# Attention and two MLPs in one kernel: the matmuls of constants get a PSUM bank of their own, the weights' scratch shrinks to one bank, and the ranks are set anew

## The chip, the cores and the metric

The kernel runs on one core of a Trainium2 chip. The metric is the device time of one execution in microseconds. The engines are TensorE (PE in the rows), its weight loads (PEld), VectorE (DVE), ScalarE (ACT), GpSimd (POOL) and SyncE (SP, which issues most DMAs).

## The reference

Softmax attention over 4 batches, 8 heads, 576 positions and a head size of 64, in which scores below the row's maximum minus `tau` are dropped before the exponential. Its output, 2304 tokens by 512, goes through two MLPs of width 2048, one after the other, with no residual.

```python
scores = scale * np.matmul(q, k.transpose(0, 1, 3, 2))
thresh = np.max(scores, axis=-1, keepdims=True) - tau
scores = np.where(scores >= thresh, scores, -1000000000.0)
attn = softmax(scores)                       # exp(scores - max) / (sum + 1e-9)
x = (attn @ v) as [tokens, heads * head_dim]
h = x @ w_in1;  x = (h * np.clip(h + 3.0, 0.0, 6.0) / 6.0) @ w_out1
h = x @ w_in2;  x = (h - np.tanh(h)) @ w_out2
```

Everything is float32. The kernel splits a float32 operand into two halves of 16 bits and adds up three products, so what TensorE does in layer 1 and 2 is three times the plain number of matmuls.

## The kernel before

**Stages.** Up to about 530 us attention runs in 144 units. A unit is one head and 128 queries (a rest of 64 queries for two heads makes a unit of its own): four score matmuls (line 717) into a tile of two PSUM banks, the row maxima on VectorE (722), the exponential on ScalarE (724), the threshold (727 on ScalarE for the first 30 units, 730 on VectorE after that), the mask on VectorE (733). For two or three units together the result is cut into high and low halves (738 on ScalarE, 744 on GpSimd), turned by a DMA transpose (747) and multiplied with the values (770). The transposing of keys, queries and values on TensorE (589, 605, 656) and their splitting (612, 614, 619, 621, 654 to 672) go on beside it. When half a batch (256 or 320 tokens) is through, its x is normed (797 to 807), its scale found (`x_scale`, 819 to 823: a transpose, a maximum, a spread to all partitions, and a power of two on VectorE at 475 to 479), and it is transposed and split (852 to 857).

Layer 1 runs over such halves of batches in passes: a pass is one half of a batch and one half of the 2048 hidden columns. `PASSES` lists ten passes that run beside attention; six more (`ENDING`) follow it, and then layer 2. A pass has eight hidden blocks (516, gates at 870 to 885) and four output blocks (958). A pass needs its weights: each of 16 weights of the first half of hidden columns is loaded into one of three staging tiles (426, 431), made absolute on ScalarE (437) and clamped on GpSimd (441), and put together from 64 bits on VectorE in three steps (446, 449, 452) that use a PSUM bank of `R_m` as scratch. When all eight of a kind are there, their norms give the scale (1028 to 1038), and they are split into halves (1047, 1049). The second half of the weights goes the same way later.

**Order.** No engine's order is written by hand. Each piece of work is a task with an engine, a guessed duration, what it depends on and a key. `Plan.issue` plays through the program with these durations: each engine that is free takes the task with the lowest key among those that are ready, and the instructions are issued in the order so found. On the chip each engine works through its list in that order and waits where data isn't there. So a key is a rank, not a time. Unit u has the key T0 + 3.0 u + 0.8 min(u, 4). Pass p starts at a key of its own: at least FO x 3.0 behind the key of the last unit that it needs (plus five), and at least FW behind the pass before it. The first weights have T0 + 3.0 (W0 + 0.8 n), their scaling WAL later and WAP apart; the second half's weights begin with unit WB0.

**PSUM.** There are eight banks: two tiles of two banks for scores (`R_s`), two banks for transposes and small products (`R_tp`), and two banks `R_m`, which layer 1 uses for its products and which the weights use as scratch. `R_m` is a free ring: a task that needs a bank takes whichever of the two is free by the plan's times.

**Fillers.** When the plan finds TensorE free with nothing ready, before `until` (470 us by the plan's time), and TensorE's planned work of late is under a share of 0.55, it puts in two matmuls of constants (line 688). They write the columns 288 to 511 of the two banks of the score tile that was written last; scores take 0 to 287 of each. Each instruction's waits follow from the tiles that it touches, so a filler waits for the readers of that tile and they for it. At the start 24 of them are issued at once.

Of the kernel before, what the change touches and what calls it, by code (L numbers as in the profile page):

```python
# [15 lines left out]
BF16 = mybir.dt.bfloat16  # L16
# [57 lines left out]
class Plan:  # L74
# [13 lines left out]
    def add(self, eng, dur, key, fn, r=(), w=(), after=(), xfer=0.0, hold=False, slack=0.0, port=None):  # L88
        r, w = ([getattr(b, "of", b) for b in x] for x in (r, w))
        deps = dict.fromkeys(after)  # L90
        for b in r:
            deps.update(dict.fromkeys(b.writers))
        t = Task(eng, dur, key, fn, deps, xfer, hold, slack, eng == "pool" if port is None else port)
        t.w = w
        users = dict.fromkeys((*r, *w))
        t.free = [b for b in users if b.ring.free]
        for b in users:
            b.users.append(t)
        for b in w:
            b.writers.append(t)  # L100
        self.tasks.append(t)
        return t
# [97 lines left out]
def t_act(n, sbuf=False, scalars=False):  # L200
    return 0.05 + n / 1200.0 + 0.043 * sbuf + 0.094 * scalars
# [6 lines left out]
def t_pool(n):  # L208
    return 0.14 + n * 0.0021
# [3 lines left out]
def attention_moe_moe_kernel(  # L213
# [41 lines left out]
    SH = S // 2  # L255
# [11 lines left out]
    plan = Plan()  # L267
    add = plan.add

    LAG = 4  # L270
    STEP, SLOW, KNEE = 3.0, 0.8, 4
    LK, LQ, LV, LD = 5, 2, 1, 4
    XL, FO = 1, 6.1
    FW = 35.6
    W0, WS, WO = 7.2, 0.8, -2.0
    PVK, GK, RK = -7.0, -5.0, -2.6
    T2O = 0.0
    PASSES = [(0, 0, 0), (0, 1, 0), (1, 0, 0), (0, 0, 1), (1, 1, 0), (0, 1, 1), (2, 0, 0), (1, 0, 1), (2, 1, 0), (3, 0, 0)]
    CLAMP, LOD = True, (8, 8)
# [4 lines left out]
    F0, EK, CL, P2L, CF = 2.0, 4.0, 0.2, 22.0, 1.0  # L284
    NF, SF, PACE, PREP, PW, TK = 18, 14, 11.0, 2, 55.0, 40
    PK, PREP0 = (100.0, 90.0), 1
    T0 = 10.2
    WB0, WBS, WBD, WBL, WBP = 34, 2, 0.8, 6.1, 3.0
    WAL, WAP = 7.0, 1.82
    ZU, TAIL = 30, 3  # L290
    ST, SB, CS = 5.3, 2.9, 0.0
    SHARE, UNTIL, FIRST_FILL = 0.55, 470.0, 24
    LG, LX, LR = 0.0, 0.0, 0.0


# [29 lines left out]
    ones = const.tile([128, 128], F32, name="ones")  # L325
# [18 lines left out]
    def at_ring(*a):  # L344
        at_rings.append(ring(*a))
        return at_rings[-1]

    R_s = at_ring(ps_s, 2, [128, 2, 512], F32, "s")
# [47 lines left out]
    R_m = Ring(2, lambda i: ps_m.tile([128, 512], F32, tag=f"m{i}", name="m"), free=True)  # L396
# [142 lines left out]
    NU = len(units)  # L539
# [139 lines left out]
        return QT[b, g, j].t[:, part, h % 2, c % 2 * 128:c % 2 * 128 + 128]  # L679

    GT, XT = {}, {}
    scored = [None]

    def filler(n=2):

        spare = scored[0].t[:, :, SH:512]
        for i in range(n):
            nc.tensor.matmul(  # L688
                spare[:, i % 2], ones.bitcast(BF16)[:, 0:128], ones.bitcast(BF16)[:, 0:512 - SH], start=True, stop=True)

    def sum_group(u):

        b, g, j, h, c = units[u]
        if h is None:
            return [u]
        return [x for x in (u - 1, u, u + 1) if 0 <= x < NU and units[x][:4] == (b, g, j, h)]

    def softmax(u, key):

        b, g, j, h, c = units[u]  # L700
        ps, z = R_s.new(), R_z.new()
        hs = (h,) if h is not None else (2 * j, 2 * j + 1)
        us = sum_group(u)
        if u == us[0]:
            GT[u] = R_e.new(), R_pp.new(), R_pt.new()
        (e, pp, pt), n = GT[us[0]], u - us[0]
        s = lambda: ps.t[:, :, 0:SH]
        ex = lambda: e.t[:, n, :].rearrange("p (a s) -> p a s", a=2)

        def scores():  # L710
            scored[0] = ps
            if u == NU - 1:
                plan.until = 0.0
            ops = [(queries(b, g, j, x, c, part), KS[b, j].t[:, x % 2]) for x in hs for part in range(2)]
            for i, (l, ks) in enumerate(ops):
                for half in range(2):
                    nc.tensor.matmul(  # L717
                        ps.t[:, half, 0:SH], l, ks[:, half * SH:(half + 1) * SH], start=i == 0, stop=i == len(ops) - 1,
                    )

        add("pe", 0.53 * len(hs), key, scores, r=[KS[b, j], QT[b, g if h is not None else "l", j]], w=[ps])
        add("dve", 0.69, key, lambda: nc.vector.tensor_reduce(  # L722
            out=z.t[:, 0:1], in_=s(), axis=AX.XY, op=ALU.max, negate=True), r=[ps], w=[z])
        exp = add("act", 0.66, key, lambda: nc.scalar.activation(  # L724
            out=ex(), in_=s(), func=ACTF.Exp, bias=z.t[:, 0:1]), r=[ps, z], w=[e])
        if u < ZU:
            add("act", 0.2, key, lambda: nc.scalar.activation(
                out=z.t[:, 1:2], in_=z.t[:, 0:1], func=ACTF.Identity, scale=-1.0, bias=tau_b[:, 3:4]), r=[z], w=[z], after=[exp])
        else:
            add("dve", 0.15, key, lambda: nc.vector.tensor_scalar(  # L730
                out=z.t[:, 1:2], in0=z.t[:, 0:1], scalar1=-1.0, scalar2=tau_b[:, 1:2],
                op0=ALU.mult, op1=ALU.subtract), r=[z], w=[z])
        add("dve", 0.74, key, lambda: nc.vector.scalar_tensor_tensor(  # L733
            out=ex(), in0=s(), scalar=z.t[:, 1:2], in1=ex(), op0=ALU.is_ge, op1=ALU.mult),
            r=[ps, e, z], w=[e])
        if u == us[-1]:
            w = len(us)
            high = add("act", t_act(w * S, sbuf=True), key, lambda: nc.scalar.activation(  # L738
                out=pp.t[:, 0:w, 0:S], in_=e.t[:, 0:w, :], func=ACTF.Copy), r=[e], w=[pp])

            for src, dst in ((slice(SM, S), slice(S, S + LF)), (slice(0, SM), slice(S + LF, 2 * S))):
                ln = w * (src.stop - src.start)
                eng, dur, queue = ("pool", t_pool(ln), nc.gpsimd) if u < NU - TAIL else ("dve", t_dve(ln), nc.vector)
                add(eng, dur, key, lambda src=src, dst=dst, queue=queue: queue.tensor_tensor(  # L744
                    out=pp.t[:, 0:w, dst], in0=e.t[:, 0:w, src], in1=pp.t[:, 0:w, src], op=ALU.subtract),
                    r=[e], w=[pp], after=[high])
            add("dma", 0.65, key, lambda: nc.sync.dma_start_transpose(
                out=pt.t[:, 0:w].rearrange("p u k n -> p (u k) n"), in_=pp.t[:, 0:w].rearrange("p u s -> p (u s)")),
                r=[pp], w=[pt], xfer=1.63 * w, hold=True)
        return pt  # L750
# [65 lines left out]
    def x_scale(b, g, key):  # L816

        hb = 2 * b + g
        x = add("dve", 0.15, key, lambda: nc.vector.tensor_reduce(
            out=xtop[:, hb:hb + 1], in_=xsq[:, hb, 0:2 + g], axis=AX.X, op=ALU.max), after=x_done[b, g])  # L820
        x = highest(xtop[:, hb:hb + 1], one[0:1, hb % 4:hb % 4 + 1], key + 0.1, [x], R_tp, LX)
        x = everywhere(one[0:1, hb % 4:hb % 4 + 1], key + 0.1, [x], R_tp, 0.45, lambda bank: root(
            bank, xpow[:, 0, hb:hb + 1], xpow[:, 1, hb:hb + 1]), LX)
        x_scaled[b, g] = x

    def x_unscale(b, g, half, key):

# [139 lines left out]
    with tc.manual_schedule():  # L967
# [7 lines left out]
        nc.vector.tensor_scalar(out=tau_b[:, 3:4], in0=tau_b[:, 1:2], scalar1=-1.0, scalar2=None, op0=ALU.mult)  # L975
        nc.vector.memset(three[:, 0:1], 3.0 * GS)
        nc.vector.memset(xsq.rearrange("p b i -> p (b i)"), 0.0)
        plan.idle, plan.until, plan.share = filler, UNTIL, SHARE
        ps0 = R_s.new()

        def first():
            scored[0] = ps0
            filler(FIRST_FILL)

        add("pe", 0.19 * FIRST_FILL, -100.0, first, w=[ps0])
        for t in vt_t:
            for i in range(2):
                nc.gpsimd.memset(t[:, i, :, :, D:D + 1].rearrange("p h c d -> p (h c) d"), 1.0 - i)
# [16 lines left out]

        when = lambda u: T0 + STEP * u + SLOW * min(u, KNEE)
        W1, staged, w_scaled, w_found = {}, {}, {}, {}
# [82 lines left out]
        for u in range(NU + LAG + XL + 4):  # L1090
# [8 lines left out]
            if w_parts[0]:  # L1099
                kind, m = w_parts[0].pop(0)  # L1100
                n = 2 * MH - len(w_parts[0]) - 1
                key = T0 + STEP * (W0 + WS * n + WO * (kind == "o"))
                weight(0, kind, m, key, 0.8, slack=ST, scratch=R_m, cs=CS)
# [7 lines left out]
        start = 0.0  # L1111
# [9 lines left out]
        for b, g, half in PASSES:  # L1121
            if half == 0:
                start = max(start, when(last_unit[b, g] + LAG + XL) + FO * STEP)
                x_rounds(b, g, start - FO * STEP)
            layer1(b, g, half, start, FW)
            start += FW
        for b, g in last_unit:
# [47 lines left out]
        key = T2  # L1175
        steps, hid, before, count = [], [], {}, [0]
        for x, (b, g, half) in enumerate(ENDING):
# [14 lines left out]
            for ms in groups:  # L1192
                ps = (R_m, R_h)[count[0] % 2].new()
# [3 lines left out]
                for a, m in enumerate(ms):  # L1197
                    turn[:] = [add("pe", P, key + a * P, lambda a=a, m=m, ps=ps, n=n, half=half, xT=xT, c=len(ms): mm3(
                        ps.t[:, a * n:(a + 1) * n], in_pairs(W1[half, "i", m], xT.t, slice(0, n)),
                        first=a == 0, last=a == c - 1),  # L1200
# [296 lines left out]
        for idx, st in enumerate(order2):  # L1497
# [36 lines left out]
            if p < NP2:  # L1534
# [6 lines left out]
                ps, k_, then = piece(0, "A11", "X11")  # L1541
                s1 = keep(ps, k_)
                then()
                ps, k_, then = piece(1, "S2", "T2")
# [3 lines left out]
                ps, k_, then = piece(2, "A12", "X21")  # L1548
# [3 lines left out]
                ps, k_, then = piece(3, "S1", "T1")  # L1552
# [3 lines left out]
                ps, k_, then = piece(4, "S4", "X22")  # L1556
# [3 lines left out]
                ps, k_, then = piece(5, "S3", "T3")  # L1560
# [4 lines left out]
                ps, k_, then = piece(6, "A22", "T4")  # L1565
# [4 lines left out]
            else:  # L1570
                a, b = R_m.new(), R_m.new()
# [55 lines left out]
```

## Time and profile before

| | us |
|---|---|
| median of 3 runs | 1082.66 |
| these runs | 1080.37 to 1085.33 |
| the profiled execution | 1079.7 |
| its span, first to last instruction | 1077.9 |
| TensorE busy | 1016.5 (94%) |
| VectorE busy | 808.4 (75%) |
| ScalarE busy | 723.9 (67%) |
| GpSimd busy | 355.2 (33%) |
| fillers on TensorE, 374 matmuls | 52.4 |

Busy time is an average over stages. To read it for this change the span has to be cut: the stage up to the first pass of layer 1 (118 us), the stretch in which attention and layer 1 run together, and the rest, in which TensorE alone is left. TensorE's busy time includes the fillers, so real work is the one less the other. An idle time that a row names in front of an instruction is put down to the instruction on another engine that came last before it.

### The profile page before, as it was taken

To read this page: it belongs to the slowest core of one execution; us is meant where nothing else is said; L and a number is where in the kernel's file an instruction comes from. 1 tells how busy PE (TensorE), PEld (TensorE's weight loads), DVE (VectorE), ACT (ScalarE), POOL (GpSimd) and SP (SyncE) were. 2 spreads that over 40 slices of the span, in tenths; PEclk is the share of its full clock that TensorE was granted. 3 is DMA by queue.
4 is the path that set the end of the run, shared out by engine and by line. 5 is a ranking of instruction groups with operands and counts; after the bars stand their busy time and mean duration, and the time that the engine had idled before them with its cause. 6 is when DMAs were issued, how large, how long until landed. Compare 5 with 4: busy or idle time off the path is not lost.

```text
span 1077.9 us, 24007 instructions
## 1 busy us (share of the span) xinstructions
PE 1016.5 (94%) x9293; PEld 780.7 (72%) x9293; DVE 808.4 (75%) x1625; ACT 723.9 (67%) x1347; POOL 355.2 (33%) x377
## 2 busy tenths in 40 slices
PE   7667996999999999999999999999999999999998
PEld 5556885778988788898786787776576666666664
DVE  5878899989688577886547896478987796784664
ACT  6757787897998677886555774457756674574332
POOL 3544546786867465765320000000001111111000
PEclk9998999999999999999999999999999999999999
DMA  7788779998768766786648664133234856574335
GB/s 184 169 191 176 148 165 199 209 206 168 150 151 166 149 135 141 140 147 140 132 146 290 215 217 138 58 104 134 90 124 132 206 133 109 127 128 52 87 90 144
DMA packets 284946, 161.48 MB, mean 150 GB/s; under 512 B 203168, under 2 KB 261024, under 8 KB 284832
## 3 DMA queue, kind: packets, MB, share of 16 engines
q1 hardware_dynamic: 279024, 150.25, 56.3%
q0 software_dynamic: 5184, 9.44, 6.4%
q8 instruction: 73, 1.20, 0.5%
q14 instruction: 41, 0.34, 0.1%
q10 hardware_dynamic: 624, 0.26, 0.1%
HBM read 76.02 MB, written 41.42 MB: 109 GB/s over the span
## 4 chain that ended last, share of the span: by engine, by line
PE 79%; DVE 9%; ACT 6%; DMA 3%; issue 2%; POOL 1%; SPq 0%; ACTq 0%; DVEq 0%
PE ya L516 23%; PE m L516 22%; PE h L516 9%; PE m L958 8%; PE s L717 6%; PE tp L770 5%; PE s L688 3%; DVE z L722 2%; PE tp L589 2%; ACT e L724 2%; DMA pt<-pp 2%; DVE e L733 1%; DVE ks L614 1%; ACT wo L1047 1%; DVE m L449 1%
## 5 line engine op out<-in xcount | busy, mean ns | idle before, releaser
L516 PEld LDWEIGHTS <-wo 128*128 128x128 f16 x2112 | 201.2, 98 | 57.4 <-issue 1.7
L744 POOL TENSOR_TENSOR pp<-e,pp 128x128 f16<-128x128 f32 (+3 forms) x156 | 180.5, 1177 | 120.1 <-issue 57.5
L516 PE MATMUL ya<-wo,g 128*128 128x512 f16 x864 | 205.4, 379 | 2.5 <-DVE g L882 1.3
L516 PEld LDWEIGHTS <-wi 128*128 128x128 f16 x1536 | 149.7, 98 | 39.6
L516 PE MATMUL m<-xT,wo 128*128 128x256 f16 (+1 forms) x1248 | 168.8, 285 | 2.5 <-DVE t L872 1.5
L1447 POOL DMA_DIRECT2D po<-o x36 | 31.3, 876 | 410.6 <-ACT o L1441 410.6
L516 PEld LDWEIGHTS <-g 128*128 128x128 f16 x864 | 83.5, 98 | 82.3 <-DVE g L882 3.1
L733 DVE SCALAR_TENSOR_TENSOR e<-s,z,e 128x576 f32<-128x576 f32 x144 | 116.5, 812 | 29.0 <-ACT e L724 19.6
L722 DVE TENSOR_REDUCE z<-s 128x1 f32<-128x576 f32 x144 | 107.7, 751 | 35.4 <-PE s L717 31.6
L958 PE MATMUL m<-g,wo 128*128 128x256 f16 (+1 forms) x960 | 128.7, 284 | 1.3 <-ACT y L903 0.6
L724 ACT ACTIVATE e<-s,z 128x576 f32<-128x576 f32 x144 | 105.6, 737 | 30.9 <-DVE z L722 19.1
L878 ACT ACTIVATE g<-t 128x512 f16<-128x512 f32 (+1 forms) x168 | 94.3, 565 | 41.9 <-DVE t L1414 24.6
L958 PEld LDWEIGHTS <-wo 128*128 128x128 f16 x960 | 89.3, 98 | 22.9 <-issue 1.8
L717 PE MATMUL s<-ks,q 128*128 128x288 f32 x512 | 101.3, 322 | 4.0 <-DVE e L733 3.7
L738 ACT ACTIVATE pp<-e 128x1152 f16<-128x1152 f32 (+1 forms) x80 | 85.0, 1062 | 15.9 <-DVE e L733 15.1
L516 PE MATMUL m<-x,wi 128*128 128x256 f16 x768 | 94.9, 273 | 0.0
L1412 ACT ACTIVATE t<-t,hid_s 128x512 f32<-128x512 f32 x72 | 51.6, 719 | 62.8 <-DVE t L1403 62.3
L770 PE MATMUL tp<-vt,pt 128*128 128x65 f16 (+1 forms) x2240 | 83.4, 195 | 10.0 <-ACT x L777 2.9
L770 PEld LDWEIGHTS <-pt 128*128 128x128 f16 (+1 forms) x2240 | 78.5, 101 | 18.4 <-issue 13.0
L717 PEld LDWEIGHTS s<-ks,q 128*128 128x128 f32 x512 | 74.6, 193 | 10.0 <-DVE e L733 5.8
L688 PE MATMUL s<-ones 128*128 128x224 bf16 x374 | 52.4, 283 | 26.9 <-ACT e L724 15.0
L516 PE MATMUL ya<-g,wo 128*128 128x320 f16 (+1 forms) x576 | 77.5, 290 | 0.0
(166 smaller groups left out, 1631.2 us busy)
## 6 DMA issues: line engine op xcount, KB each, us to landing
st<-in_moe_w_in_dram SPq DMA_DIRECT2D x32, 512.0 KB, 4.6
st<-in_moe_w_out_dram SPq DMA_DIRECT2D x32, 512.0 KB, 4.6
po<-o POOLq DMA_DIRECT2D x36, 256.0 KB, 4.2
ys<-y SPq DMA_DIRECT2D x32, 160.0 KB, 2.1
y<-ys SPq DMA_DIRECT2D x9, 512.0 KB, 5.3
po<-o SPq DMA_DIRECT2D x18, 256.0 KB, 2.0
o<-po SPq DMA_DIRECT2D x18, 256.0 KB, 3.3
kr<-in_k_dram SPq DMA_DIRECT2D x16, 256.0 KB, 3.8
```

What stands on the lines that cost most here:

```text
L516: nc.tensor.matmul(ps, l[a], r[b], start=first and t == 0 and i == 0, stop=last and t == 2 and i == n - 1,)
L688: nc.tensor.matmul(spare[:, i % 2], ones.bitcast(BF16)[:, 0:128], ones.bitcast(BF16)[:, 0:512 - SH], start=True, stop=True)
L717: nc.tensor.matmul(ps.t[:, half, 0:SH], l, ks[:, half * SH:(half + 1) * SH], start=i == 0, stop=i == len(ops) - 1,)
L722: add("dve", 0.69, key, lambda: nc.vector.tensor_reduce(out=z.t[:, 0:1], in_=s(), axis=AX.XY, op=ALU.max, negate=True), r=[ps], w=[z])
L724: exp = add("act", 0.66, key, lambda: nc.scalar.activation(out=ex(), in_=s(), func=ACTF.Exp, bias=z.t[:, 0:1]), r=[ps, z], w=[e])
L733: add("dve", 0.74, key, lambda: nc.vector.scalar_tensor_tensor(out=ex(), in0=s(), scalar=z.t[:, 1:2], in1=ex(), op0=ALU.is_ge, op1=ALU.mul ...
L738: high = add("act", t_act(w * S, sbuf=True), key, lambda: nc.scalar.activation(out=pp.t[:, 0:w, 0:S], in_=e.t[:, 0:w, :], func=ACTF.Copy), ...
L744: add(eng, dur, key, lambda src=src, dst=dst, queue=queue: queue.tensor_tensor(out=pp.t[:, 0:w, dst], in0=e.t[:, 0:w, src], in1=pp.t[:, 0: ...
L770: nc.tensor.matmul(pv.t[0:m, w_ * (D + 1):(w_ + 1) * (D + 1)], pt.t[:, n, blk, rows], vv, start=o == 0, stop=o == len(ops) - 1)
L878: hi = add("act", t_act(n, sbuf=True), key, lambda: nc.scalar.activation(out=gh(), in_=t(), func=ACTF.Copy, scale=GS2 if far else 1.0), r= ...
L958: prev = [add("pe", t_half(n, 1), kd, lambda o=o, l=l, r=r, m=m, s=s, ps=ps, gt=gs[m // 2]: nc.tensor.matmul(ps.t[:, 0:n], W1[half, "o", m ...
L1412: add("act", t_act(2 * NB, sbuf=True, scalars=True), key, lambda: nc.scalar.activation(out=s_(), in_=h.t, func=ACTF.Tanh, scale=c), r=[h], ...
```

## The change

The fillers write columns 0 to 223 of one tile `unread`, which is taken from `R_m` at the start and which nobody reads. It is held until a last task, which issues one more filler, sets `until` to 0 and runs once the scale of the first half batch's x is found; no filler is put in after it. Until then `R_m` has one bank left, so the weights' three steps share that one. A group of constants is set anew. Among them T0 is a summand of all keys of units, weights and passes.

```diff
-    LK, LQ, LV, LD = 5, 2, 1, 4
-    XL, FO = 1, 6.1
-    FW = 35.6
-    W0, WS, WO = 7.2, 0.8, -2.0
-    PVK, GK, RK = -7.0, -5.0, -2.6
+    LK, LQ, LV, LD = 5, 2, 2, 4
+    XL, FO = 1, 9.2
+    FW = 34.4
+    W0, WS, WO = 7.3, 0.8, -2.0
+    PVK, GK, RK = -6.8, -5.0, -2.6
...
-    T0 = 10.2
-    WB0, WBS, WBD, WBL, WBP = 34, 2, 0.8, 6.1, 3.0
-    WAL, WAP = 7.0, 1.82
+    T0 = 8.4
+    WB0, WBS, WBD, WBL, WBP = 36, 2, 0.8, 6.1, 2.2
+    WAL, WAP = 6.2, 0.87
...
-    SHARE, UNTIL, FIRST_FILL = 0.55, 470.0, 24
+    SHARE, FC, FIRST_FILL = 0.55, 224, 24
...
-    scored = [None]
-
     def filler(n=2):
 
-        spare = scored[0].t[:, :, SH:512]
         for i in range(n):
             nc.tensor.matmul(
-                spare[:, i % 2], ones.bitcast(BF16)[:, 0:128], ones.bitcast(BF16)[:, 0:512 - SH], start=True, stop=True)
+                unread.t[:, 0:FC], ones.bitcast(BF16)[:, 0:128], ones.bitcast(BF16)[:, 0:FC], start=True, stop=True)
...
         def scores():
-            scored[0] = ps
-            if u == NU - 1:
-                plan.until = 0.0
...
         x_scaled[b, g] = x
+        if (b, g) == (0, 0):
+            def last():
+                plan.until = 0.0
+                filler(1)
+
+            add("pe", 0.1, key, last, w=[unread], after=[x])
...
-        plan.idle, plan.until, plan.share = filler, UNTIL, SHARE
-        ps0 = R_s.new()
-
-        def first():
-            scored[0] = ps0
-            filler(FIRST_FILL)
-
-        add("pe", 0.19 * FIRST_FILL, -100.0, first, w=[ps0])
+        plan.idle, plan.until, plan.share = filler, 1000.0, SHARE
+        unread = R_m.new()
+        add("pe", 0.19 * FIRST_FILL, -100.0, lambda: filler(FIRST_FILL), w=[unread])
```

## Rows read from the trace of the kernel before

**Rows 1.** Stretches: length, busy PE, PEld, DVE, ACT, POOL (instructions), clock, DMA, GB/s.
```profile
20.00:120.00 100.00, 72.27 (x800) 62.35 (x799) 85.12 (x142) 69.75 (x136) 51.18 (x55) 0.93 0.76 168
160.00:200.00 40.00, 29.53 (x349) 24.40 (x348) 35.82 (x79) 32.91 (x61) 24.84 (x26) 1.00 0.89 205
260.00:540.00 280.00, 277.60 (x3214) 234.71 (x3211) 204.84 (x437) 220.37 (x415) 172.69 (x169) 1.00 0.71 144
540.00:1077.90 537.90, 529.36 (x3782) 368.55 (x3780) 383.89 (x768) 305.69 (x567) 36.91 (x41) 1.00 0.50 136
```

**Rows 2.** The same stretches, line 688 alone: length, busy PE, PEld, clock, DMA, GB/s.
```profile
20.00:120.00 100.00, 32.38 (x238) 23.03 (x236) 0.93 0.76 168
120.00:160.00 40.00, 1.31 (x12) 1.16 (x12) 1.00 0.76 156
160.00:200.00 40.00, 6.61 (x48) 4.22 (x48) 1.00 0.89 205
200.00:260.00 60.00, 3.33 (x26) 2.34 (x26) 1.00 0.94 203
```

**Rows 3.** Chain of waits (start, us, what), then TensorE's timeline, around 115 us.
```profile
110.79 0.16 DVE xpow L479
...
117.98 2.78 PE L516 MATMUL m<-xT,wo 128*128 128x256 f16 x24
```

**Rows 4.** Waits of TensorE, 20 to 120 us: total, times, longest.
```profile
PE s L688 <- ACT e L724: 10.4, 10, 1.7
PE s L688 <- DVE z L722: 8.6, 7, 2.0
```

**Rows 5.** Lines of VectorE, 20 to 120 us: busy, mean ns, idle before, releasers.
```profile
L733 DVE SCALAR_TENSOR_TENSOR e<-s,z,e 128x576 f32<-128x576 f32 x27 | 21.9, 812 | 5.9 <-PE s L688 4.4 <-ACT z L727 1.3
L722 DVE TENSOR_REDUCE z<-s 128x1 f32<-128x576 f32 x26 | 19.5, 750 | 5.4 <-PE s L717 3.4 <-PE s L688 2.0
```

**Rows 6.** Waits of VectorE, 120 to 260 us: total, times, longest.
```profile
DVE z L722 <- PE s L688: 1.2, 2, 0.7
DVE ks L614 <- PE s L717: 0.7, 1, 0.7
```

**Rows 7.** Chain of waits, 20 to 95 us: shares by line.
```profile
by line: PE s L688 23.3%; DVE z L722 12.4%; ACT e L724 11.2%; PE s L717 8.9%; issue 8.3%; PE tp L770 4.8%; DVE m L449 4.3%; DVE e L733 4.0%; ACT pp L738 3.6%; DVE ks L614 2.5%; ACT vr L668 2.2%; DVE rx L797 2.0%; ACT z L727 2.0%; DVE wo L45
```

**Rows 8.** Timeline of VectorE: start, us, line, operation.
```profile
69.50 0.69 DVE L446 TENSOR_SCALAR m<-wo 128x512 int32<-128x512 int32 x1
70.09 0.68 DVE L452 SCALAR_TENSOR_TENSOR wo<-st,m 128x512 uint32<-128x512 uint32 x1
...
96.94 0.68 DVE L446 TENSOR_SCALAR m<-wo 128x512 int32<-128x512 int32 x1
97.65 0.70 DVE L449 SCALAR_TENSOR_TENSOR m<-st,m 128x512 int32<-128x512 int32 x1
```

**Rows 9.** Line 449 alone, 0 to 140 us: least, median, most ns; first and last start.
```profile
L449 DVE SCALAR_TENSOR_TENSOR m<-st,m x16: 684/686/697, 23.1 to 129.7; 128x512 int32<-128x512 int32 x16
```

**Rows 10.** Timeline of TensorE ahead of the second part of pass 1; idle before in brackets.
```profile
142.05 1.05 PE L770 MATMUL tp<-vt,pt 128*64 128x65 f16 x28 [1.17 <-ACT x L777]
143.03 1.59 PE L958 MATMUL m<-g,wo 128*128 128x256 f16 x13
```

**Rows 11.** Timeline of TensorE: two groups of four score matmuls.
```profile
66.93 0.76 PE L717 MATMUL s<-ks,q 128*128 128x288 f32 x4
...
76.20 1.31 PE L717 MATMUL s<-ks,q 128*128 128x288 f32 x4
```

**Rows 12.** 160 to 190 us: the stretch as in rows 1, then two lines of TensorE.
```profile
160.00:190.00 30.00, 19.96 (x241) 16.54 (x240) 27.70 (x61) 23.04 (x43) 16.85 (x17) 1.00 0.90 201
...
L717 PE MATMUL s<-ks,q 128*128 128x288 f32 x36 | 6.9, 317 | 1.3 <-DVE e L733 1.3
...
L770 PE MATMUL tp<-vt,pt 128*128 128x65 f16 (+1 forms) x120 | 4.5, 194 | 2.8 <-DVE ks L614 2.8
```

## The prediction

> **What bounds the kernel now.** I read the stretches first: busy time of each engine from 20 us to the end [rows 1]. The reader is to see two regimes. From 260 to 540 us TensorE is busy 277.60 of 280 us and after that 529.36 of 537.9: there the end is set by the sum of TensorE's work, and anything that lets that work begin earlier moves the end by as much. From 20 to 120 us TensorE is busy 72.27 of 100 us, and the next view, the same stretches for the matmuls of constants alone (fillers, line 688) [rows 2], says that 32.38 of these are fillers; 39.9 us are real. From 160 to 200 us it is 29.53, 6.61 of it filler, so 22.9 real. The first product of layer 1 runs at 117.98 us [rows 3], so what counts up to there is how fast attention and the preparing of weights go, and VectorE is the fullest engine (85.12 of 100). The change lies in this regime; its gain is what VectorE gets back of its 14.9 idle us, its price whatever holds up the same chain in another way.
>
> Third, the waits. In 20 to 120 us fillers waited 10.4 us for the exponentials and 8.6 us for the row maxima [rows 4]: a filler writes the free columns of the very tile of scores that ScalarE and VectorE are reading. TensorE takes its matmuls in order, so the next unit's scores, which have a tile of their own, stood behind these waits. The other side of it is VectorE's list [rows 5]: its masking step waited 4.4 us for a filler, its maximum 2.0 us for a filler and 3.4 us for scores. From 120 to 260 us the like is 1.2 and 0.7 us [rows 6]. Last, the chain of waits from 20 to 95 us puts 23.3% of 75 us, 17.5 us, on fillers [rows 7]. That is the largest share of any line, and on a line that computes nothing.
>
> **The change, part by part.** The sum is made against the profiled execution, 1079.7 us (its span of 1077.9 and 1.8 around it). It is 3.0 us under the median of 1082.66, so I add 3.0 at the end.
>
> *Fillers get a bank that nobody reads.* Their 19.0 us of waiting [rows 4] goes, and the readers of scores no longer wait for them. TensorE's own waiting isn't the saving, since VectorE is the bound. The saving is what VectorE waited for fillers and for scores that stood behind them: 4.4 + 2.0 + 3.4 = 9.8 us [rows 5], and 1.2 + 0.7 = 1.9 us later [rows 6]. The scores may turn out to be held by something else, so the lower bound is the two rows that name a filler, 6.4 us, less what the bank costs; the upper bound is the 17.5 us of the chain [rows 7], which VectorE's idle time of 14.9 us nearly allows. I take 9.8 + 1.9 = 11.7 us, the direct rows. Next late is VectorE itself.
>
> *No filler after the scale of the first x.* That scale's last step starts at 110.79 us [rows 3]. Fillers busy after 120 us add up to 1.31 + 6.61 + 3.33 = 11.3 us [rows 2], and all of it stands where TensorE had nothing to do; taking it out gains no time by itself. The price is the clock. The granted clock was 1.00 from 160 to 190 us with fillers in [rows 12], and 0.93 from 20 to 120 [rows 1], where for a time a group of four score matmuls took 1.31 us instead of 0.76 [rows 11]: 1.2 instead of 2.4 GHz, after idle stretches of TensorE. From 160 to 190 us the score matmuls are busy 6.9 us and the products with the values 4.5 [rows 12]. All at the lower level, that is 11.4 x (1.31 / 0.76 - 1) = 8.2 us more of TensorE time. VectorE is busy 27.70 of these 30 us [rows 12], so most of it would lie beside VectorE's work; where VectorE runs out of other work, a late score adds to its 2.3 idle us. Bounds 0 and 8.2; I take 2 us, by that idle time. Should layer 1's pass 2 itself begin at the lower level, it is in the upper half of these bounds.
>
> The Trainium skill (TensorE: Matmul & The Clock Gate, Part 1: The HAM clock gate) speaks against this part: by it the low clock is the default and only activity lifts it, so that stuffing the gaps is what keeps later matmuls fast. The trace agrees in the stretch of [rows 11]; for the gap at 160 us without fillers no run here shows it. By the rule alone the term would be the 8.2 us, and rival (c) is that rule taken through the whole regime.
>
> *One scratch bank for the weights until then.* The unread tile holds one of the two banks of R_m, so the 16 weights of the first half go through the other, one at a time. Today two weights are sometimes interleaved: line 452 starts 0.59 us after another weight's 446, while in one weight the second step starts 0.71 us after the first [rows 8]. Three steps, 16 weights, 0.12 us each is at most 5.8 us, if VectorE never has anything else between two steps. It nearly always has (maxima, masks), and weights pass at (129.7 - 23.1) / 15 = 7.1 us apiece [rows 9] for some 2.1 us of steps, so one bank is free most of the time. Bounds 0 and 5.8; I take 1 us.
>
> The Trainium skill (VectorE: DVE Perf Modes, The DRAIN you can't avoid) would put the term at nothing: a chain with a semaphore after each step took as long there as one without. The rows here differ by 0.12 us, so the rows decide.
>
> *The keys.* A key is only a rank among what is ready, so the shift of T0, which all keys share, does nothing. WAL 6.2 and WAP 0.87 rank the scaling of the first weights higher. Now TensorE comes to the second part of pass 1 at 143.03 us; ahead of it stand the 12 fillers of this stretch, 1.31 us [rows 2], and 1.17 us of idle time [rows 10], together 2.5 us that are to be had. WB0 lets the second half of the weights begin two units later, about one weight less, 2.1 us of VectorE [rows 8], ahead of the x for pass 2. FO 9.2 puts pass 1 9.3 us lower in rank against attention, which works against the thin stretch from 160 to 200 us, where pass 2 waits for attention; FW 34.4 takes the shift back, 1.2 us a pass. LV loads values a unit earlier. Bounds: nothing, and the whole 10.5 us idle and 6.6 us filler of that stretch, 17.1 us [rows 1, 2]; below nothing too, since a lower rank could hold up pass 1's gates, by as much as the 2.5 us of such a wait. I take 3 us, the 2.5 and a little of the rest, because VectorE is full there.
>
> Sum: 1079.7 - 11.7 + 2 + 1 - 3 = 1068.0; with the 3.0 us, **1071 us**.
>
> **The rivals.** (a) *The stream of weights is the wall: no change.* Pass 1 needs sixteen weights, and they run from 23.1 to 129.7 us through three staging tiles [rows 9], whose loads wait for the slots and not for fillers. If that stream sets the start of layer 1's second part, attention's 9.8 us only pile up ahead of it, and what stays is the 1.9 and 2.5 us: 1082.66 - 4.4 = 1078. For it: the second part started just after these weights. Against: their steps run on the same VectorE that loses the 9.8 us.
>
> (b) *Both gaps close.* The 11.7 us and the 17.1 us of 160 to 200: 1082.66 - 28.8 = 1054. For it: the keys all push attention ahead of pass 1. Against: VectorE's 27.70 of 30 us [rows 12] leaves little to squeeze.
>
> (c) *Slower, by the clock.* Fillers that used to wait ran in the middle of a wait and broke it up [rows 4]; fillers that wait for nothing run at its start, and the silence behind them is longer. If the clock then stays at its lower level through 20 to 120 us, each of the 26 maxima there [rows 5] has its scores 0.55 us later [rows 11], 14.3 us, and 160 to 190 adds the 8.2: 1082.66 - 11.7 - 3 + 1 + 14.3 + 8.2 = 1091. It decides against the change once the granted clock of 20 to 120 us, 0.93 now, is under about 0.6. For it: 0.93 holds with the fillers where they are now. Against: the real matmuls come closer together when nothing delays them.
>
> **How the numbers follow.** Forecast 0.54, own range 1062 to 1077; (a) 0.20; (b) 0.15; (c) 0.11. What a measurement of this kernel can tell from no change is about 0.5%, 5.4 us: 1077.2 to 1088.1. Faster: forecast and (b), 0.69. Same: (a), 0.20. Slower: (c), 0.11. The range reaches down to (b) and up past (a), 1055 to 1086, which also takes in the filler term at its lower bound with the bank at its upper one, 1082.66 - 6.4 + 5.8 + 2 = 1084.
>
> **What would show it.** Right: no row in which a filler waits for the exponentials or the maxima, and none in which the masks wait for a filler; VectorE idle under 8 us in 20 to 120; the first product of layer 1 at about 108 instead of 118 us; the last score about 10 us earlier. The keys' term: no idle TensorE ahead of pass 1's second part, and 160 to 200 with over 26 us of real work. Wrong: the first product early but the second part still near 143 us (a), or score groups of 1.31 us through most of 20 to 120 (c).

## The result, and the profile after

The changed kernel took 1073.4 us (median of 4 runs, 1069.8 to 1073.9) against 1084.0 for the kernel before; the ratio is 0.9896, 95% interval 0.9857 to 0.9936. Forecast were 1071 us (1062 to 1077) and a gain of 11.7; it is 1.0%, about 11 us. The profiled execution took 1073.3 us, its span 1071.6. Times inside a kernel come from one profiled execution each. The kernel before took 1077.0 to 1088.2 us in the 26 runs beside the last four experiments, so a difference of 2 or 3 us between two such traces is not clear of noise.

The stretches of the changed kernel, as in [rows 1]:

```profile
20.00:120.00 100.00, 77.37 (x873) 65.34 (x871) 91.09 (x155) 78.21 (x154) 56.99 (x61) 0.95 0.84 186
120.00:160.00 40.00, 30.25 (x330) 26.45 (x331) 36.69 (x73) 29.12 (x55) 23.45 (x26) 0.83 0.70 158
160.00:200.00 40.00, 35.58 (x394) 29.07 (x393) 37.80 (x81) 35.69 (x66) 26.18 (x27) 1.00 1.00 198
260.00:540.00 280.00, 274.36 (x3120) 230.62 (x3118) 202.83 (x427) 215.47 (x404) 166.22 (x163) 0.99 0.69 138
540.00:1071.60 531.60, 523.32 (x3729) 364.09 (x3727) 380.88 (x757) 301.89 (x559) 34.45 (x39) 1.00 0.51 138
```

Its fillers alone (now line 685), the answer to [rows 2]:

```profile
20.00:120.00 100.00, 21.46 (x167) 15.68 (x167) 0.95 0.84 186
120.00:160.00 40.00, 0.00 (x0) 0.00 (x0) 0.83 0.70 158
```

From 20 to 120 us VectorE is idle 8.9 us instead of 14.9, and real work on TensorE is 77.37 - 21.46 = 55.9 us instead of 39.9. From 160 to 200 us real work is 35.6 instead of 22.9. Between them lies a stretch that got worse: 30.25 us of 40, at a clock of 0.83, where it was 38.03 - 1.31 = 36.7 at 1.00. The kernel before there:

```profile
120.00:160.00 40.00, 38.03 (x463) 34.36 (x462) 35.70 (x68) 33.13 (x59) 21.27 (x21) 1.00 0.76 156
```

Later stretches are much as they were.

VectorE's two lines from 20 to 120 us, the answer to [rows 5]:

```profile
L727 DVE SCALAR_TENSOR_TENSOR e<-s,z,e 128x576 f32<-128x576 f32 x29 | 23.5, 812 | 2.9 <-ACT z L721 2.3 <-ACT e L718 0.4
L716 DVE TENSOR_REDUCE z<-s 128x1 f32<-128x576 f32 x30 | 22.2, 747 | 3.7 <-PE s L711 3.7
```

TensorE's longest waits in the same stretch, the answer to [rows 4]:

```profile
PE s L711 <- DVE e L727: 10.1, 9, 2.3
PE tp L764 <- DMA pt<-pp: 2.8, 2, 2.5
```

No filler stands in these lists any more. The maxima still wait 3.7 us for scores (3.4 before), and the scores now wait 10.1 us for the masks: TensorE waits for VectorE directly. Last, the timeline of TensorE at the first product of layer 1 [rows 3], at the second part of pass 1 [rows 10], and at pass 2:

```profile
97.01 1.05 PE L516 MATMUL m<-xT,wo 128*128 128x256 f16 x8 [0.60 <-ACT wo L1042]
...
147.81 1.11 PE L589 MATMUL tp<-ident,kr 128*128 128x128 f32 x4 [4.76 <-ACT x L771]
148.72 2.55 PE L958 MATMUL m<-g,wo 128*128 128x256 f16 x11
...
173.91 2.89 PE L516 MATMUL m<-xT,wo 128*128 128x320 f16 x20
```

Pass 2 in the kernel before:

```profile
189.23 0.71 PE L516 MATMUL m<-xT,wo 128*128 128x320 f16 x4
```

From the chain of waits, what stood ahead of that second part:

```profile
142.70 4.90 ACT wo L1042 x8
```

Pass 1 begins 21 us earlier (97.0 for 118.0). Its second part begins 5.7 us later (148.7 for 143.0), behind eight scalings of weights in a row on ScalarE. Pass 2 begins 15 us earlier (173.9 for 189.2).

One view gives the end of every run below. The last x needs its scale before the rest of layer 1 can be finished; this is the last of eight transposes on line 496 (first and last start behind the comma), here of the kernel before, the changed one, and the sixth experiment:

```profile
L496 PE MATMUL tp<-ident,xtop x8: 269/272/273, 97.9 to 543.3; 128*1 128x128 f32 x8
```

```profile
L496 PE MATMUL tp<-ident,xtop x8: 270/273/277, 85.4 to 537.7; 128*1 128x128 f32 x8
```

```profile
L496 PE MATMUL tp<-ident,xtop x8: 270/272/273, 80.9 to 551.6; 128*1 128x128 f32 x8
```

Their spans end 534.6, 533.9 and 536.4 us behind it. Over all fourteen kernels it is 533.8 to 537.8, while their spans differ by 18.7 us. So nearly all is decided before that transpose, at 538 to 556 us, and a lead at one place counts only if it is still there at it. Note the first number: the sixth experiment has the earliest first scale of the three, and the latest last one.

### The profile page after: what moved, and what is told of

Same layout as the page of the kernel before. It is cut to its first block, busy times and chain, and to the rows that moved or that the text cites. A ratio compares the mean times of both kernels' runs of the same rounds, so it can differ in the third digit from the quotient of the medians.

```text
span 1071.6 us, 23700 instructions
## 1 busy us (share of the span) xinstructions
PE 1009.5 (94%) x9140; PEld 771.7 (72%) x9140; DVE 813.9 (76%) x1625; ACT 723.3 (68%) x1347; POOL 353.9 (33%) x377
## 4 chain that ended last, share of the span: by engine, by line
PE 75%; DVE 11%; ACT 7%; DMA 3%; issue 3%; POOL 1%; SPq 0%; ACTq 0%; POOLq 0%; DVEq 0%
PE ya L516 23%; PE m L516 20%; PE m L958 9%; PE h L516 9%; PE s L711 5%; PE tp L764 5%; DVE e L727 2%; DMA pt<-pp 2%; DVE z L716 2%; PE tp L589 1%; ACT pp L732 1%; ACT e L718 1%; PE tp L1023 1%; DVE wo L452 1%; DVE ks L614 1%
## 5 line engine op out<-in xcount | busy, mean ns | idle before, releaser
L516 PE MATMUL m<-xT,wo 128*128 128x256 f16 (+1 forms) x1248 | 171.9, 287 | 6.8 <-DVE wo L452 4.4
L732 ACT ACTIVATE pp<-e 128x1152 f16<-128x1152 f32 (+1 forms) x80 | 85.1, 1064 | 22.8 <-DVE e L727 19.9
L870 ACT ACTIVATE t<-m,three,unscale 128x320 f32<-128x320 f32 (+1 forms) x76 | 51.2, 674 | 35.5 <-PE m L516 35.2
```

The lines of the kernel that those rows point to most:

```text
L516: nc.tensor.matmul(ps, l[a], r[b], start=first and t == 0 and i == 0, stop=last and t == 2 and i == n - 1,)
L870: add("act", t_act(n, scalars=True) + 0.05, key, lambda: nc.scalar.activation(out=t(), in_=ps(), func=ACTF.Relu, bias=three[:, 0:1], scale ...
```

## The experiments

Twelve kernels, each with the kernel before run beside it on the same chip; ratios are to that.

**1. The bank with the old ranks.** The changed kernel with all its constants of ranks set back.

```diff
-    LK, LQ, LV, LD = 5, 2, 2, 4
-    XL, FO = 1, 9.2
-    FW = 34.4
+    LK, LQ, LV, LD = 5, 2, 1, 4
+    XL, FO = 1, 6.1
+    FW = 35.6
...                       # W0, PVK, T0, WB0, WBP, WAL, WAP likewise
```

Expected: 

> The changed kernel with all constants of the ranks as they were before: the fillers have their bank, the weights one scratch bank, fillers end at the first scale of x. Theory (the bank brings the gain, the ranks 3 us): 1074 to 1079 us, no wait of a filler for ScalarE or VectorE, first product of layer 1 near 105 us instead of 118. Rival (the ranks bring it, the bank only makes room): 1080 to 1087 us, though the waits are gone.

Measured: 1086.3 us, ratio 1.0052 (1.0027 to 1.0077): slower than before, and in the rival's range. Its stretches of 20 to 120 and of 148 to 187 us, then the second of these in the kernel before:

```profile
20.00:120.00 100.00, 77.00 (x942) 67.16 (x941) 92.94 (x162) 76.44 (x149) 54.61 (x59) 1.00 0.91 188
...
148.00:187.00 39.00, 26.57 (x245) 22.58 (x246) 34.52 (x72) 27.91 (x52) 22.95 (x23) 0.62 0.85 192
```

```profile
148.00:187.00 39.00, 29.41 (x338) 25.03 (x337) 35.75 (x73) 30.49 (x56) 22.94 (x24) 1.00 0.87 195
```

VectorE's maxima from 20 to 120 us, as in [rows 5], and the timeline of TensorE at the first product, at the second part of pass 1 and at pass 2:

```profile
L716 DVE TENSOR_REDUCE z<-s 128x1 f32<-128x576 f32 x28 | 20.9, 749 | 0.7 <-PE s L711 0.4
```

```profile
104.74 1.47 PE L516 MATMUL m<-xT,wo 128*128 128x256 f16 x12
...
126.58 1.58 PE L958 MATMUL m<-g,wo 128*128 128x256 f16 x13
...
186.72 2.30 PE L516 MATMUL m<-xT,wo 128*128 128x320 f16 x12
```

Up to pass 1 all came as the theory had it: no filler waits, the maxima wait 0.4 us for scores, VectorE is idle 7.1 us instead of 14.9, and the first product runs at 104.7 us, 13.3 earlier (11.7 were forecast). That is more than the 7.8 us that VectorE got back; where the rest comes from wasn't settled. The second part of pass 1 begins at 126.6, 16 us earlier. But pass 2 begins at 186.7 instead of 189.2, and what was won is gone: pass 1 is over about 148 us, and from there TensorE has only attention, is busy 26.6 of 39 us and is granted a clock of 0.62. At the last transpose this kernel is 3.6 us behind (546.9 for 543.3), and 3.2 us more come after it. The bank does what it was meant to do up to pass 1, and isn't enough.

**2. The ranks with the old bank.** The kernel before with the new constants, all but WB0 and WBP. All of them with the old bank weren't tried.

```diff
-    XL, FO = 1, 6.1
-    FW = 35.6
+    XL, FO = 1, 9.2
+    FW = 34.4
...                       # LV, W0, PVK, T0, WAL, WAP likewise
```

Expected: 

> The kernel before with the new ranks, all but the start of the second half of the weights (unit 34 kept): the fillers still write into the scores' tile, the weights have two scratch banks. Theory: 1078 to 1082 us, VectorE still waits some 8 us for fillers between 20 and 120 us. Rival (the ranks bring the gain): 1071 to 1076 us.

Measured: 1085.9 us, ratio 1.0041 (1.0020 to 1.0062). Both theories miss: these ranks alone cost. Fillers still wait 17.2 us for their readers from 20 to 120 us:

```profile
PE s L688 <- DVE z L722: 9.3, 8, 1.7
PE s L688 <- ACT e L724: 7.9, 9, 1.6
```

VectorE itself waits only 2.2 us for fillers there, where 8 were expected, and the first product comes at 111.4 us, 6.6 earlier; but pass 2 begins at 188 us.

**3. Fillers again after the first scale of x.** In the changed kernel they go on, in the scores' tile.

```diff
-                unread.t[:, 0:FC], ones...
+                unread.t[:, 0:FC] if free_bank[0] else scored[0].t[:, i % 2, SH:SH + FC], ones...
...
-                plan.until = 0.0
                 filler(1)
+                free_bank[0] = False
+                plan.until = 470.0
```

Expected: 

> The changed kernel, but after the first scale of x the fillers go on in the scores' tile as before, up to 470 us of the plan. It keeps TensorE's clock up in the stretch from 120 to 160 us, where it was 0.83 in the changed kernel. If the lower clock there costs what the sum put down for it (2 us or more): 1069 to 1071.5 us and a clock of 0.95 or more in that stretch. If it costs nothing because VectorE and the weights hold that stretch: 1072 to 1075 us, with the clock up all the same. If late fillers get in the way: over 1076 us.

Measured: 1074.1 us, ratio 0.9929 (0.9901 to 0.9957), not told apart from the changed kernel. The clock came up, the work got no further, as the stretch of 120 to 160 us shows:

```profile
120.00:160.00 40.00, 32.46 (x418) 28.67 (x416) 36.64 (x74) 29.41 (x56) 23.58 (x25) 0.96 0.80 162
```

VectorE's 36.64 us is the 36.69 of the changed kernel, and the second part of pass 1 begins at 148.9 us as against 148.7. Of TensorE's 32.46 us 8.1 are fillers. Here the low clock cost nothing that shows, unless the late fillers cost as much as the clock gave back, which these runs can't tell apart.

**4. One scratch bank alone.** The kernel before with one bank of `R_m` held until the first scale of x; the fillers stay where they were.

```diff
+        held = R_m.new()
+        add("pe", 0.1, -100.0, touch, w=[held])
...
+        if (b, g) == (0, 0):
+            add("pe", 0.1, key, touch, w=[held], after=[x])
```

Expected: 

> The kernel before, but one bank of the two that the weights use as scratch is held by a tile that nobody reads until the first scale of x, as in the changed kernel; fillers stay in the scores' tile. It is the cost of the one scratch bank alone. By the sum's term it is 1 us (1083 to 1086); by its upper bound 5.8 us (1088 to 1090); if the weights are the wall of pass 1's second part and one bank makes them late, that part starts later than 143 us by as much as the last weight.

Measured: 1085.6 us, ratio 1.0033 (1.0014 to 1.0051), 3.6 us. The place that the expectation named was wrong: the weights weren't late (the sixteenth's last step at 120.4 instead of 130.4 us, the second part of pass 1 at 138 instead of 143). Pass 2 begins at 191 us, 1.6 later, and the last transpose of line 496 runs at 548.9 us, 5.6 later. Where between these the cost arises wasn't settled.

**5. The first experiment with late fillers,** by the edit of the third.

Expected: 

> The bank with the old ranks, as in the run with the bank alone, and fillers in the scores' tile after the first scale of x. There TensorE had a clock of 0.65 from 160 to 200 us while it waited for the x of pass 2. If the low clock is what ate the 13 us won up to pass 1: 1072 to 1077 us, pass 2 starting near 180 us. If it is the order (pass 1 runs early and then pass 2 waits for attention, which is no further than before): 1080 to 1086 us with the clock up, and pass 2 starting at 184 to 190.

Measured: 1075.5 us, ratio 0.9956 (0.9941 to 0.9970), against 1.0052 without late fillers. Its pass 2, from the timeline, and the stretch of 148 to 187 us:

```profile
180.93 0.71 PE L516 MATMUL m<-xT,wo 128*128 128x320 f16 x4
```

```profile
148.00:187.00 39.00, 31.82 (x334) 26.67 (x332) 33.11 (x74) 28.69 (x53) 21.59 (x21) 0.82 0.88 193
```

So with the old ranks fillers in that gap are worth 1%. The clock there is 0.82 instead of 0.62, and pass 2 begins 5.8 us sooner, which speaks for the low clock as what ate part of the 13 us; since the plan's order of other work moves a little with each filler, the clock alone isn't shown.

**6 and 7. One group of ranks set back at a time.** In the changed kernel, first the passes' (FO 6.1, FW 35.6), then all of the weights'.

```diff
-    XL, FO = 1, 9.2
-    FW = 34.4
+    XL, FO = 1, 6.1
+    FW = 35.6
```

Expected of the passes': 

> The changed kernel with the passes' two constants as before (FO 6.1, FW 35.6), the rest new. If the passes' lower rank is what carries the gain through (attention goes ahead of pass 1, so that x of pass 2 is sooner): 1079 to 1086 us, the 36th row maximum later than 128 us and pass 2 starting after 180. If the weights' ranks carry it: 1071 to 1076 us, pass 2 near 174.

```diff
-    W0, WS, WO = 7.3, 0.8, -2.0
-    WB0, WBS, WBD, WBL, WBP = 36, 2, 0.8, 6.1, 2.2
-    WAL, WAP = 6.2, 0.87
+    W0, WS, WO = 7.2, 0.8, -2.0
+    WB0, WBS, WBD, WBL, WBP = 34, 2, 0.8, 6.1, 3.0
+    WAL, WAP = 7.0, 1.82
```

Expected of the weights': 

> The changed kernel with the weights' constants as before (W0 7.2, WB0 34, WBP 3.0, WAL 7.0, WAP 1.82), the passes' new. If the passes' rank carries the gain: 1071 to 1077 us. If the weights' ranks do, the later start of the second half above all: 1080 to 1086 us, with more of the second half's weights done by 190 us than in the changed kernel and pass 2 later than 174.

Measured: the passes' set back 1089.1 us, 1.0077 (1.0051 to 1.0102); the weights' 1078.1, 0.9977 (0.9960 to 0.9994), which lies between the ranges of its two theories. More of the weights are through by 190 us (22 against 20), as the second had it, but pass 2 begins sooner, at 170 us. The passes' rank carries the most, but not by the place that I named: pass 2 begins at 173 us with the old one too. What falls back is attention. Row maxima (line 716) in three stretches, first of the changed kernel, then with the passes' rank set back (the number of instructions is in brackets; one that lies across a border is counted on both sides):

```profile
0.00:120.00 120.00, 23.00 (x32) 0.94 0.84 191
120.00:200.00 80.00, 16.89 (x23) 0.91 0.85 178
200.00:340.00 140.00, 29.22 (x39) 0.99 0.82 177
```

```profile
0.00:120.00 120.00, 24.46 (x33) 0.96 0.85 195
120.00:200.00 80.00, 14.27 (x19) 0.82 0.75 163
200.00:340.00 140.00, 26.17 (x36) 0.96 0.75 166
```

They are level at 120 us; by 340 us 93 maxima have begun against 88. Passes 2 to 4 begin at 174, 234 and 287 us against 173, 232 and 285, as early; then pass 5 at 325 against 333, pass 7 at 415 against 428. Pass 5 is the first that needs the fourth x, and there the loss shows: the transpose on line 496 for it, first of the changed kernel, then with the passes' rank set back, is 19 us later, where that of the third x was still level (225 and 224 us):

```profile
294.91 0.27 PE L496 MATMUL tp<-ident,xtop 128*1 128x128 f32 x1
```

```profile
314.25 0.27 PE L496 MATMUL tp<-ident,xtop 128*1 128x128 f32 x1 [0.95 <-DVE ks L614]
```

So I read it thus: early passes that go ahead of attention are paid for by the later ones, which wait for their x.

**8. No fillers in the changed kernel,** but the first 24.

```diff
-    SHARE, FC, FIRST_FILL = 0.55, 224, 24
+    SHARE, FC, FIRST_FILL = 0.0, 224, 24
```

Expected: 

> The changed kernel without fillers but for the first 24 and the last one. If fillers earn their place by the clock: a granted clock under 0.8 from 20 to 120 us and 1076 to 1090 us (rival c of the prediction priced a low clock through that stretch at 14 us). If VectorE hides what a low clock costs there: 1072 to 1075 us.

Measured: 1090.2 us, ratio 1.0092 (1.0070 to 1.0113). First product at 115.9 us instead of 97.0. The stretch, and from the timeline of TensorE a group of score matmuls and the first product:

```profile
20.00:120.00 100.00, 65.07 (x568) 55.54 (x568) 83.36 (x141) 68.59 (x134) 49.51 (x54) 0.67 0.79 168
```

```profile
64.32 1.30 PE L711 MATMUL s<-ks,q 128*128 128x288 f32 x4 [0.49 <-DVE e L727]
...
115.86 0.75 PE L516 MATMUL m<-xT,wo 128*128 128x256 f16 x4
```

The clock is 0.67, score groups take 1.30 us, and VectorE is idle 16.6 us. In this kernel the fillers are worth 2%. Rival (c) had priced a low clock up to pass 1 at 14 us; here the first product comes 19 us later. Experiment 10 shows that this is not the clock alone.

**9. The passes' rank set back, with late fillers,** by the edits of the sixth and the third.

Expected: 

> The changed kernel with the passes' constants as before (FO 6.1, FW 35.6), which came to 1.0077 of the kernel before, and with fillers in the scores' tile after the first scale of x. If the passes' new rank pays because it keeps TensorE in work, and so its clock up, once the fillers are gone: 0.992 to 0.998 of the kernel before, the clock over 0.95 from 240 to 320 us (0.83 to 1.00 in slices there without late fillers). If the rank pays by the order itself: 1.004 to 1.010 with the clock up.

Measured: 1089.6 us, ratio 1.0066 (1.0041 to 1.0092), at a clock of 0.99 from 240 to 320 us. My theory that the rank pays by keeping up the clock fell: late fillers, which gave 1% to the old ranks as a set, give nothing here. The loss is one of order; attention stays behind, with 86 maxima begun by 340 us.

**10. No fillers in the kernel before.**

```diff
-    SHARE, UNTIL, FIRST_FILL = 0.55, 470.0, 24
+    SHARE, UNTIL, FIRST_FILL = 0.0, 470.0, 24
```

Expected: 

> The kernel before without fillers but for the first 24. If fillers in the scores' tile gave by the clock about what they cost by their waits up to the first pass: the first product of layer 1 at 114 to 122 us (118 with them) at a granted clock under 0.8 from 20 to 120 us; the end 1 to 1.3% later by what the late ones did for the clock. If they were a net gain there: first product later than 124 us. If a net loss: earlier than 112.

Measured: 1080.7 us, ratio 0.9980 (0.9959 to 1.0001). The stretch, and from the timeline the first product of layer 1:

```profile
20.00:120.00 100.00, 68.61 (x612) 58.08 (x612) 88.86 (x150) 73.30 (x142) 53.00 (x59) 0.68 0.83 181
```

```profile
109.09 3.22 PE L516 MATMUL m<-xT,wo 128*128 128x256 f16 x20
```

At a clock of 0.68, lower than any in [rows 1], the first product comes 9 us earlier than with fillers. In the scores' tile they cost more up to pass 1 than the clock gave. The end I had wrong: it isn't 1% later, but the same. Beside experiment 8 this says two things more. Neither kernel has fillers, both have a clock of 0.67 or 0.68, and yet the old ranks with two scratch banks end 1.1% (0.9980 against 1.0092) sooner than the new ranks with one; so the 2% of experiment 8 is what this order loses without fillers, and not the clock alone. And against a kernel that simply has no fillers the whole change gains 0.8% (0.9896 against 0.9980), about 9 us.

**11 and 12. The weights' ranks apart.** The changed kernel with W0, WAL and WAP set back and WB0 36 and WBP 2.2 kept; and the changed kernel with WB0 38.

```diff
-    WB0, WBS, WBD, WBL, WBP = 36, 2, 0.8, 6.1, 2.2
+    WB0, WBS, WBD, WBL, WBP = 38, 2, 0.8, 6.1, 2.2
```

Expected of the first half's: 

> The changed kernel with the first half's weights ranked as before (W0 7.2, WAL 7.0, WAP 1.82); the second half keeps its later start (WB0 36, WBP 2.2). With the second half's constants old as well it was 0.9977 of the kernel before. If the later start of the second half is what counts among the weights' ranks: 0.988 to 0.993. If the first half's: 0.995 to 1.000.

Expected of the later start: 

> The changed kernel with the second half of the weights starting two units later still (WB0 38). If VectorE ahead of pass 2 and 3 is still the bound, another weight less there: 0.984 to 0.990 of the kernel before, 1 to 5 us better than the changed kernel. If these weights then hold up pass 4, which is the first to need them: 0.992 to 1.000, with pass 4 starting later than 287 us.

Measured: 1073.6 us, 0.9923 (0.9897 to 0.9948), and 1075.3 us, 0.9944 (0.9923 to 0.9966). The scaling of the first weights, to which my sum gave its 2.5 us, shows no effect clear of noise. The second half's constants do: 0.9977 with them set back, 0.9923 without, and the intervals don't meet. Two units later still is no better: pass 4 begins at 276 us, so the weights didn't hold it up, though the second theory said so, but pass 5 begins at 327 instead of 325, and nothing is won.

No kernel here was clearly better than the changed one.

## Why the prediction was right, point by point

The value, the sign and the range were right, the working only in part, and that the sum met the time is luck. The bank with its two prices was to gain 11.7 - 2 - 1 = 8.7 us and by itself lost 0.5%, about 6 us (experiment 1); the ranks were to gain 3 us and on top of it gained 17. The two errors, some 14 us each way, cancel.

**The bank.** The term was 11.7 us at the start of layer 1. Without the new ranks 13.3 were measured (experiment 1). The waits of [rows 5] went as forecast, 9.8 us down to 0.4, but VectorE's idle time was cut by only 7.8 us, so that the 13.3 lie near the 11.7 is in part chance. In the changed kernel the 6.4 us that name a filler went, while the wait of the maxima for scores stayed (3.7 us for 3.4): scores now wait 10.1 us for the masks, the case for which the lower bound was set. What failed is the step "anything that lets that work begin earlier moves the end by as much": from there to the end it isn't kept. Pass 2 waits for another x, of 13.3 us 2.5 arrive there, and none at the end.

**First product.** I said 108 us; it came at 97.0. The bank alone gives 104.7, 13.3 us, and the new ranks alone 111.4, 6.6 us (experiment 2); together that is 19.9 of the 21.0. The passes', the first weights' and all of the weights' ranks were each set back with the first product still at 93 to 97, so no one of these groups is needed for it; of the other constants LV and PVK weren't run apart. Of the other signs, VectorE was to be idle under 8 us and is idle 8.9, and the last score was to come 10 us earlier and comes 6 (522.6 for 528.6).

**The end of fillers.** 2 us were put down. With the new ranks it is not to be seen (experiment 3); with the old ones some 10 us (1.0052 against 0.9956). The bounds were 0 and 8.2, and the second case lies above them. Which case holds wasn't settled: with the passes' ranks alone set back, late fillers brought nothing either (experiment 9). The fall of the clock itself came, to 0.83, but at 120 to 160 us, not at 160 to 190. The Trainium skill (TensorE: Matmul & The Clock Gate, Part 1: The HAM clock gate) has the low clock come back once activity ends; the traces agree, with this 0.83 and with 0.67 where no fillers ran (experiment 8).

**One scratch bank.** 1 us against 3.6 measured alone, inside its bounds. That the weights' steps were rarely held up fits, since the sixteenth weight came 10 us earlier with one bank; where the cost arises stays open.

**The ranks.** This is the term that was mis-sized. I took 3 us; with the bank in place they are 1.0052 - 0.9896 = 1.6%, 17 us, and without it, WB0 and WBP aside, less than nothing (1.0041). With the bank the second half's constants were worth 0.5% (0.9977 against 0.9923); if they were worth as much without it, all the ranks with the old bank would come to about 0.999, an estimate that no run tested. "TensorE comes to the second part of pass 1": the 2.5 us there turned into 4.76 us of idle time and a start 5.7 us later, behind a sixteenth weight at 134.8 instead of 130.4 us. That doesn't show as a loss, because attention got ahead in that time: pass 2 begins 15 us sooner. The thin stretch of 160 to 200 did fill, to 35.6 us of real work where over 26 were asked for. I had the direction of FO right ("works against the thin stretch") and its reach wrong: its gain is still there at pass 7, with attention ahead. That the order does it, and not the clock, is shown by experiment 9.

**The rivals.** (a) gave 1078, and its sign was met: the first product early, the second part of pass 1 not (148.7 us). Yet the time was 1073, so its premise fails that what attention wins only piles up ahead of that second part. Nor is the stream of weights a wall: in experiment 1, with the same staging tiles and scratch bank, the sixteenth weight is through at 109.3 us and the second part begins at 126.6. (b), both gaps closed, is what happened at 160 to 200 us, and the lead of 15 us at pass 2 shrank to 4 at pass 4; the span is 6.3 us shorter in the two profiles. (c) needed a clock under 0.6 from 20 to 120 us; it was 0.95 with fillers that don't wait, and 0.67 without them (experiment 8).

## What to carry to other kernels

A wait that is removed is worth its size only up to the next meeting of two streams; ask what the stream that got ahead will wait for there, and give the time to the one that is late. A change of a resource and a change of ranks can each lose alone and win together, as here (with WB0 and WBP left out of the ranks alone), so test the pair, and test each part against the pair, not only against the start. Find the event that has a nearly fixed distance to the end, here the last scale of x, and read every edit by when that event comes.

## What the runs showed of the hardware

Matmuls that only keep the clock up have a price by where they write. In a tile that others read they gave a clock of 0.93 instead of 0.68 from 20 to 120 us and still brought the first product 9 us later (118.0 against 109.1); in a bank that nobody reads they gave 0.95 instead of 0.67 and brought it 19 us earlier (97.0 against 115.9). The two kernels differ in ranks and scratch banks too, and taking fillers out moves the order of other work, so these figures hold for fillers in their kernel and not for the clock alone. And a granted clock of 0.83 over 40 us cost nothing that could be measured against 0.96 with late fillers (experiment 3), where VectorE was busy 36.7 of them.
